# The opening of a spectral + gated-linear-unit kernel: first weights prepared by GpSimd, rows normalised by ScalarE, left-over columns split before the transpose

## The chip, the cores and the metric

The kernel runs on one core of one Trainium2 chip. The metric is the device time of one launch in microseconds (us), the median of the runs. The engines are named as in the profile: PE is TensorE (PEld its weight loads), DVE is VectorE, ACT is ScalarE, POOL is GpSimd, and SP is SyncE, whose queue issues nearly all DMAs. Each engine works through its own list of instructions in order; a list waits where its next instruction waits.

## What is computed

```python
x = A_x                                   # (1, 2048, 576)
xn = _layernorm(x, axis=-1)               # eps 1e-5, no scale or shift
g = einsum("bsd,df->bsf", xn, w_gate)     # 576 x 4608
u = einsum("bsd,df->bsf", xn, w_up)
glu = einsum("bsf,fd->bsd", sigmoid(g) * u, w_down)
spec = irfft2(rfft2(xn) * (w_r + 1j * w_i))
out = x + spec + glu
```

## The kernel before

The 2048 rows are 16 tiles of 128 rows (`NT`), taken in two passes of 8 tiles (`PAIRS`). In each pass the 4608 hidden columns are 36 units of 128 (`NF`), so there are 72 units. A unit multiplies the normalised rows with its gate and up columns by Strassen's scheme (Winograd's form): the 576 columns of x are two halves of 288 (`HD`), a pass has two halves of four tiles (512 rows, `CW`), and 7 products (`PRODS`) stand for 8. Every operand is split into a rounded high part and a low part (fp32r), so a product is 7 matmuls (`STEPS`): of the 288 columns two blocks of 128 with high and low part, and a left-over block of 32 columns (`REM`) whose high, high and low parts lie one below the other in 96 partitions (`KR`).

**Weights.** In pass 0 `make_w(f)` builds the seven 288x128 weight combinations of a unit from four raw blocks: `load_raw` (8 DMAs, L199 and L200), ACT rounds to the high part (L205, three blocks, then two and two), DVE forms the sums (L218, L220, L221) and the low parts (L207 and L209, the latter for the left-over 32 partitions). The result goes to `wsp` in DRAM, from where pass 1 reads it (`get_w`).

**Rows.** `stats` gives mean and 1/deviation of a tile (bn_stats, a square root on ACT or Newton steps, L263 to L282, on 128x1 values); `norm` (L285) is a DVE operation. `stage(p, m)` makes, for the tiles m and m+4, the seven 288-column combinations `xs`: norm twice, an ACT copy that repeats the 32 left-over columns (L307), two sums on DVE (L309, L311) and two on POOL (L310, L312). `fill(p, k, mm)` transposes combination k of two stages into `X`: 6 PE transposes (L322), an ACT copy of the high parts with 768 elements a partition (L325), and the low parts by two DVE operations (L326; L328 for the left-over columns, 32 partitions).

**Order.** The opening (L629 to L656) sends the loads of tiles 0 and 4, the identity matrices, the raw weights of unit 0, the other six tiles and the raw weights of unit 1, all from SP; then it stages m = 0, weights 0, m = 1, 2, 3, with the fills of the first half after m = 1 and unit 0 in two halves of 256 rows. `xs` has two buffers, so stages 2 and 3 reuse those of 0 and 1 when their fills are through. A scheduler places each engine's instructions; the code gives their priority. From unit 1 on, PE runs products with the down-projections (`down`, tile `po`, L598) between them. At the end of unit 35 `stage_pair` stages the four pairs of pass 1 (all four buffers at once), and `fill_ahead` fills `X` anew beside unit 36 (L678); the phases of the spectral part run beside pass 1 (L365 to L492).

Names in the profile: `xs` staged rows, `px` the transposes' PSUM tiles, `pA`, `pB`, `pE` the products' PSUM banks, `raw`, `tt`, `w` the weights, `acc` a tile of x that also takes the output, `rs` and `rstd` the statistics.

Of the kernel before, what the change touches and what calls it, by code (L numbers as in the profile page):

```python
# [9 lines left out]
F32 = mybir.dt.float32  # L10
# [6 lines left out]
P = 128  # L17
# [112 lines left out]
def spectral_glu_kernel(ctx: ExitStack, tc: tile.TileContext, x, w_r, w_i, w_gate, w_up, w_down, out):  # L130
# [3 lines left out]
    def f32(ap):  # L134
        return ap.bitcast(F32)
# [48 lines left out]
    def room(k):  # L184
        fp.close()
        R["pool"] = pool = fp.enter_context(tc.tile_pool(name=f"p{k}", bufs=1, reuse_waits="tile"))
        return pool
# [11 lines left out]
                nc.sync.dma_start(raw[:, b, :KT, :], v[h, :KT * P, cols].rearrange("(k p) f -> p k f", p=P))  # L199
                nc.sync.dma_start(raw[:, b, KT, :], v[h:h + 1, KT * P:, cols].to_broadcast([4, REM, P]))  # L200

    def parts(w, src, i, n):

        o = w[:, i:i + n]
        nc.scalar.activation(o[:, :, :3, :], src, AF.Copy)  # L205
# [3 lines left out]
        nc.vector.tensor_tensor(o[r, :, KT, :], src[r, :, KT, :], f32(o[r, :, KT, :]), op=OP.subtract)  # L209
        yield  # L210

    def make_w(f):
        raw = RAW[f]
        WS[f] = w = wpool.tile([P, NX, 5, P], F32R, tag="w", name=f"w{f}", bufs=2)
        tt = R["pool"].tile([P, 4, 3, P], F32, tag="tt", name=f"tt{f}", bufs=1)
        g = parts(w, raw[:, 1:], 0, 3)
        next(g)
        nc.vector.tensor_tensor(tt[:, :2], raw[:, :2], raw[:, 3::-3], op=OP.subtract)  # L218
        yield
        nc.vector.tensor_tensor(tt[:, 2], raw[:, 1], tt[:, 0], op=OP.subtract)  # L220
        nc.vector.tensor_tensor(tt[:, 3], raw[:, 2], tt[:, 2], op=OP.subtract)  # L221
        yield
        next(g)
        yield
        for i in (0, 2):
            yield from parts(w, tt[:, i:i + 2], 3 + i, 2)
# [29 lines left out]
    def load_x(dst, t, eng=None):  # L256
        for i, r in enumerate(rows(x, t)):
            (eng or nc.sync).dma_start(dst[i * N1:(i + 1) * N1, :D], r)

    def stats(src, t, pool, table=False):  # L260
        st = pool.tile([P, 2, 6], F32, tag="st", name=f"st{t}", bufs=2)
        for i in range(2):
            nc.vector.bn_stats(st[:, i, :], src[:, i * HD:(i + 1) * HD])  # L263
        nc.vector.bn_aggr(mv[:, t, :], st.rearrange("p a b -> p (a b)"))
        rs = pool.tile([P, 4], F32, tag="rs", name=f"rs{t}", bufs=2)
        ve, r0, w0, w1 = (rs[:, i:i + 1] for i in range(4))
        nc.vector.tensor_scalar(ve, mv[:, t, 1:2], EPS, None, op0=OP.add)
# [9 lines left out]
        nc.vector.tensor_scalar(ve, ve, -0.5, None, op0=OP.mult)  # L277
        for k in range(steps):
            nc.vector.tensor_tensor(w0, r0, r0, op=OP.mult)
            nc.vector.tensor_tensor(w0, w0, ve, op=OP.mult)  # L280
            o = rstd[:, t:t + 1] if k == steps - 1 else r0
            nc.vector.scalar_tensor_tensor(o, w0, 1.5, r0, op0=OP.add, op1=OP.mult)  # L282

    def norm(o, a, t):
        nc.vector.tensor_scalar(o, a, mv[:, t, 0:1], rstd[:, t:t + 1], op0=OP.subtract, op1=OP.mult)  # L285
# [2 lines left out]

    def stage(p, m, bufs):

        pool = R["pool"]
        XS[m] = xs = pool.tile([P, NX, (KT + 1) * P], F32, tag="xs", name=f"xs{p}_{m}", bufs=bufs)
        A11, A12, A21, A22, S1, S2, S4 = (xs[:, i] for i in range(NX))
        for i in range(2):
            t = p * TPP + i * TPC + m
            b = xs[:, 2 * i:2 * i + 2, :HD]
            if p:
                for k, r in enumerate(rows(x, t)):
                    nc.sync.dma_start(b[k * N1:(k + 1) * N1], r.rearrange("s (a d) -> s a d", a=2))
        yield  # L300
        for i in range(2):
            t = p * TPP + i * TPC + m
            b = xs[:, 2 * i:2 * i + 2, :HD]
# [3 lines left out]
        nc.scalar.activation(rem[:, :, 1:], rem[:, :, :1].to_broadcast([P, 4, 3, REM]), AF.Copy)  # L307
        yield
        nc.vector.tensor_tensor(S1, A21, A22, op=OP.add)  # L309
        nc.gpsimd.tensor_tensor(A21, A11, A21, op=OP.subtract)  # L310
        nc.vector.tensor_tensor(S2, S1, A11, op=OP.subtract)  # L311
        nc.gpsimd.tensor_tensor(S4, A12, S2, op=OP.subtract)  # L312
        yield

    def fill(p, k, mm):

        i = XA[PRODS[k][1]]
        cols = slice(2 * mm * P, (2 * mm + 2) * P)
        pt = pair(f"px{p}_{k}_{mm}")
        for j in range(2):  # L320
            for q in range(KT + 1):
                nc.tensor.transpose(pt[:, j, q * P:(q + 1) * P], XS[2 * mm + j][:, i, q * P:(q + 1) * P], idf)  # L322
        v = pt[:, :, :3 * P].rearrange("p j (q s) -> p q j s", q=3)
        o = X[:, i, :, cols].rearrange("p q (j s) -> p q j s", j=2)
        nc.scalar.activation(o[:, :3], v, AF.Copy)  # L325
        nc.vector.tensor_tensor(o[:, 3:], v[:, :KT], f32(o[:, :KT]), op=OP.subtract)  # L326
        r = slice(2 * REM, 3 * REM)
        nc.vector.tensor_tensor(o[r, KT], v[r, KT], f32(o[r, KT]), op=OP.subtract)  # L328

    def new_acc(p, m):  # L330
        t = p * TPP + m
        acc[t] = accp.tile([P, D], F32, tag=f"acc{m}", name=f"acc{t}")
        load_x(acc[t], t)

    def phase1b(t):
        pool, cf = R["pool"], R["cf"]
# [185 lines left out]
    def unit(u, beside, cols=slice(0, CW), tiles=None):  # L522
# [15 lines left out]
        def prod(i):  # L538
            b, ka, kb = PRODS[i]
            for j, (sx, sw) in enumerate(STEPS):  # L540
                k = KR if sw == KT else P
                nc.tensor.matmul(bank[b], w[:k, WB[kb], sw, :], X[:k, XA[ka], sx, cols], start=b not in seen and j == 0,  # L542
                                 stop=j == len(STEPS) - 1, skip_group_check=b in seen)
            seen.add(b)

# [93 lines left out]
    b0 = ps.tile([P, CW], F32, tag="bB", name="b0")  # L639
    for i in range(CW // P):  # L640
        nc.tensor.matmul(b0[:, i * P:(i + 1) * P], idr, idr, start=i == 0, stop=i == CW // P - 1, skip_group_check=True)
    mk = make_w(0)
    for m in range(TPC):
        for i in (m, TPC + m):
            stats(acc[i], i, R["pool"], table=True)
        sg = stage(0, m, 2)
        for _ in sg:
            pass
        if m == 0:
            for _ in mk:  # L650
                pass
        if m == 1:
            for k in range(NX):
                fill(0, k, 0)
        if m == 3:
# [28 lines left out]
    for u in range(LAST):  # L684
# [1 line left out]

        spots = {3: 1, 4: 2, 5: 1} if f % G == 0 else {1: 1, 3: 1, 4: 1, 5: 1}
        if u + 1 < LAST:
            make = make_w(u + 1) if u + 1 < NF else get_w(u + 1)
        wd = make_d(u) if u < NF else get_d(u)  # L690
        if 2 <= u < 2 + TPP:
            sides.append(later_stats(TPP + u - 2))
# [21 lines left out]
                aside()  # L714

        if u == 0:
            for k in range(NX):
                fill(0, k, 1)
            unit(0, beside, slice(CW // 2, CW), tiles)
        else:  # L720
            unit(u, beside)
# [35 lines left out]
```

## Time and profile before

| | |
|---|---|
| median of three runs | 1492.02 us (1490.39 to 1492.04) |
| the profiled execution's own time | 1491.86 us |
| its span, from the first to the last instruction | 1490.1 us |
| PE busy in the span | 1449.1 us (97%) |
| DVE busy, ACT busy, POOL busy | 959.8, 577.5 and 21.4 us |
| mean granted TensorE clock | 0.994 |

A timeline row reads: start in us from the span's first instruction, duration in us, engine, line, operation, output<-inputs, then forms (partitions x elements of one partition), the number of merged instructions, and in brackets the engine's idle time ahead of it with what ended it. A row of a view by stretches gives for each engine the busy time and the number of instructions, then the granted clock (1.00 is full), the DMA engines' busy share and GB/s. A row of a view by groups ends in "busy us, mean ns of one | idle before".

### The profile page before, as it was taken

To read this page: it belongs to the slowest core of one execution; us is meant where nothing else is said; L and a number is where in the kernel's file an instruction comes from. 1 tells how busy PE (TensorE), PEld (TensorE's weight loads), DVE (VectorE), ACT (ScalarE), POOL (GpSimd) and SP (SyncE) were. 2 spreads that over 40 slices of the span, in tenths; PEclk is the share of its full clock that TensorE was granted. 3 is DMA by queue.
4 is the path that set the end of the run, shared out by engine and by line. 5 is a ranking of instruction groups with operands and counts; after the bars stand their busy time and mean duration, and the time that the engine had idled before them with its cause. 6 is when DMAs were issued, how large, how long until landed. Compare 5 with 4: busy or idle time off the path is not lost.

```text
span 1490.1 us, 21470 instructions
## 1 busy us (share of the span) xinstructions
PE 1449.1 (97%) x8229; PEld 1276.4 (86%) x8229; DVE 959.8 (64%) x1628; ACT 577.5 (39%) x963; POOL 21.4 (1%) x36
## 2 busy tenths in 40 slices
PE   3899999999999999999999999999999999999998
PEld 3788888888888888887888888888888889899987
DVE  7988977776777777767465555456566544554544
ACT  3544433333344433334343434343444333433321
POOL 1100000000000000011000000000000000000000
PEclk9899999999999999999999999999999999999999
DMA  6477666666655666666874655486777576654522
GB/s 200 164 266 260 235 228 230 236 235 228 225 217 214 218 222 226 228 224 222 262 247 148 199 167 197 147 256 218 242 234 239 180 268 206 225 164 144 193 95 64
DMA packets 152630, 311.79 MB, mean 209 GB/s; under 512 B 14160, under 2 KB 79952, under 8 KB 147664
## 3 DMA queue, kind: packets, MB, share of 16 engines
q1 hardware_dynamic: 152528, 310.42, 61.3%
q8 instruction: 65, 1.06, 0.3%
q14 instruction: 37, 0.30, 0.1%
HBM read 189.98 MB, written 120.39 MB: 208 GB/s over the span
## 4 chain that ended last, share of the span: by engine, by line
PE 89%; DVE 6%; DMA 1%; issue 1%; SPq 1%; ACT 1%; DVEq 0%; ACTq 0%; POOL 0%; POOLq 0%
PE po L598 29%; PE pB L542 21%; PE pE L542 15%; PE pA L542 14%; PE pe L482 2%; PE pd L372 2%; PE pc L427 1%; PE pa L383 1%; PE px L322 1%; PE py L453 1%; PE pb L411 1%; DVE w L207 1%; DVE acc L603 1%; DVE X L326 1%; PE pz L465 0%
## 5 line engine op out<-in xcount | busy, mean ns | idle before, releaser
L598 PE MATMUL po<-wd,hh 128*128 128x288 f32 x2304 | 402.2, 296 | 4.3 <-DVE acc L603 2.6
L542 PE MATMUL pB<-X,w 128*128 128x512 f32 (+2 forms) x1533 | 392.9, 392 | 0.1
L603 DVE TENSOR_TENSOR acc<-acc,po 128x576 f32<-128x576 f32 x288 | 216.6, 753 | 261.1 <-PE po L598 260.2
L598 PEld LDWEIGHTS po<-wd,hh 128*128 128x128 f32 x2304 | 350.3, 189 | 25.0 <-DVE acc L603 3.9
L542 PEld LDWEIGHTS pB<-X,w 128*128 128x128 f32 (+1 forms) x1533 | 275.8, 189 | 48.8 <-ACT pB L549 0.7
L542 PE MATMUL pA<-X,w 128*128 128x512 f32 (+2 forms) x1022 | 264.3, 394 | 2.9 <-ACT X L325 1.8
L542 PE MATMUL pE<-X,w 128*128 128x512 f32 (+2 forms) x1022 | 264.0, 393 | 0.0
L598 PE MATMUL po<-wd,hl 128*128 128x288 f32 x1152 | 246.1, 294 | 0.0
L542 PEld LDWEIGHTS pA<-X,w 128*128 128x128 f32 (+1 forms) x1022 | 190.0, 190 | 41.8 <-ACT X L325 2.4
L542 PEld LDWEIGHTS pE<-X,w 128*128 128x128 f32 (+1 forms) x1022 | 185.7, 190 | 34.6 <-DVE y L563 0.5
L598 PEld LDWEIGHTS po<-wd,hl 128*128 128x128 f32 x1152 | 185.2, 188 | 0.2 <-DVE hl L584 0.2
L566 ACT ACTIVATE g<-pB 128x512 f32<-128x512 f32 (+1 forms) x73 | 43.1, 591 | 185.5 <-PE pB L542 185.0
L584 DVE TENSOR_TENSOR hl<-y,hh 128x1024 fp32r<-128x1024 f32 x72 | 88.0, 1222 | 27.6 <-ACT hh L583 27.4
L581 DVE TENSOR_TENSOR y<-y,g 128x1024 f32<-128x1024 f32 x72 | 88.3, 1226 | 5.9 <-DVE y L570 0.5
L562 ACT ACTIVATE v<-pB 128x512 f32<-128x512 f32 (+1 forms) x73 | 43.1, 591 | 120.6 <-PE pB L542 120.5
L583 ACT ACTIVATE hh<-y 128x1024 fp32r<-128x1024 f32 x72 | 75.5, 1048 | 9.0 <-DVE y L581 8.9
L570 DVE TENSOR_TENSOR y<-v,pE 128x512 f32<-128x512 f32 (+1 forms) x73 | 49.6, 680 | 45.3 <-PE pE L542 45.1
L205 ACT ACTIVATE w<-raw 128x1152 fp32r<-128x1152 f32 x36 | 42.0, 1167 | 88.2 <-PE pE L542 71.8
L563 DVE TENSOR_TENSOR y<-v,pE 128x512 f32<-128x512 f32 (+1 forms) x73 | 49.6, 679 | 37.3 <-ACT v L562 36.6
L556 ACT ACTIVATE v<-pB 128x512 f32<-128x512 f32 (+1 forms) x73 | 43.1, 590 | 65.6 <-PE pB L542 65.6
L549 ACT ACTIVATE pB<-pA 128x512 f32<-128x512 f32 (+1 forms) x73 | 42.0, 575 | 61.1 <-PE pA L542 61.0
L559 ACT ACTIVATE g<-pA 128x512 f32<-128x512 f32 (+1 forms) x73 | 43.2, 592 | 53.5 <-PE pA L542 53.4
(121 smaller groups left out, 1311.2 us busy)
## 6 DMA issues: line engine op xcount, KB each, us to landing
wsp<-w SPq DMA_DIRECT2D x36, 2240.0 KB
w<-wsp SPq DMA_DIRECT2D x252, 320.0 KB
wdsp<-wd SPq DMA_DIRECT2D x36, 576.0 KB
wd<-wdsp SPq DMA_DIRECT2D x36, 576.0 KB
std<-in_B_w_down SPq DMA_DIRECT2D x36, 288.0 KB
raw<-in_B_w_gate SPq DMA_DIRECT2D x72, 128.0 KB
raw<-in_B_w_up SPq DMA_DIRECT2D x72, 128.0 KB
sc<-x SPq DMA_DIRECT2D x16, 290.0 KB
```

The source lines that it names most:

```text
L542: nc.tensor.matmul(bank[b], w[:k, WB[kb], sw, :], X[:k, XA[ka], sx, cols], start=b not in seen and j == 0, stop=j == len(STEPS) - 1, skip_ ...
L556: nc.scalar.activation(v[:, 0], bank["B"], AF.Copy)
L559: nc.scalar.activation(g[:, 0], bank["A"], AF.Sigmoid)
L562: nc.scalar.activation(v[:, 1], bank["B"], AF.Copy)
L563: nc.vector.tensor_tensor(y[:, 1], v[:, 1], bank["E"], op=OP.add)
L566: nc.scalar.activation(g[:, 1], bank["B"], AF.Sigmoid)
L570: add = lambda: nc.vector.tensor_tensor(y[:, 0], v[:, 0], bank["E"], op=OP.add)
L581: nc.vector.tensor_tensor(Y, Y, G_, op=OP.mult)
L583: ends.extend([first, lambda: nc.scalar.activation(hh, Y, AF.Copy), lambda: nc.vector.tensor_tensor(hl, Y, f32(hh), op=OP.subtract)])
L584: lambda: nc.vector.tensor_tensor(hl, Y, f32(hh), op=OP.subtract)])
L598: nc.tensor.matmul(pd[:, b, :HD], l[:, c, cols], w[:, k, b * HD:(b + 1) * HD], start=g == 0 and l is hh and k == 0, stop=g == G - 1 and l ...
L603: nc.vector.tensor_tensor(a, a, pd[:, :, :HD], op=OP.add)
```

## The change

The subtractions of `make_w` for units 0 and 1 go from DVE to POOL (`eng`); all of `make_w(0)` is placed ahead of the staging. `stats` takes the two tiles of a stage together (128x2 values). In pass 0 ACT normalises (Identity with scale `rstd` and bias `nmr`, a new DVE product), and the two sums that POOL made are DVE's; in pass 1 norm stays on DVE and those two sums on POOL. The left-over columns of all seven combinations are split into high, high and low parts in `rm` ahead of the transpose (an ACT copy with 448 elements, L326, and a DVE subtraction with 224, L327), so that `fill` has four fp32 transposes and two of `rm` (L338, L339), two ACT copies (L342, L344) and one DVE operation (L343). The products read 128 instead of 96 partitions of the left-over block; POOL clears the other 32 of `X` at the start. Tiles 1 and 5 are loaded from ACT's queue, and the identity matrices behind the raw weights.

```diff
+    nmr = fix.tile([P, TPP], F32, name="nmr")
...
-    def parts(w, src, i, n):
+    def parts(w, src, i, n, eng):
         o = w[:, i:i + n]
         nc.scalar.activation(o[:, :, :3, :], src, AF.Copy)
         yield
-        nc.vector.tensor_tensor(o[:, :, 3:, :], src[:, :, :KT, :], f32(o[:, :, :KT, :]), op=OP.subtract)
+        eng.tensor_tensor(o[:, :, 3:, :], src[:, :, :KT, :], f32(o[:, :, :KT, :]), op=OP.subtract)
...
-    def make_w(f):
+    def make_w(f, eng=nc.vector):
...
-    def stats(src, t, pool, table=False):
+    def stats(srcs, t0, step, pool, table=False):
...
+        if table:
+            nc.vector.scalar_tensor_tensor(nmr[:, ts], mv[:, ts, 0], -1.0, rstd[:, ts], op0=OP.mult, op1=OP.mult)
...
-            norm(b, b if p else acc[t].rearrange("p (a d) -> p a d", a=2), t)
-
-        rem = xs[:, :4, KT * P:].rearrange("p a (q r) -> p a q r", q=4)
-        nc.scalar.activation(rem[:, :, 1:], rem[:, :, :1].to_broadcast([P, 4, 3, REM]), AF.Copy)
-        yield
+            if p:
+                norm(b, b, t)
+            else:
+                nc.scalar.activation(b, acc[t].rearrange("p (a d) -> p a d", a=2), AF.Identity,
+                                     bias=nmr[:, t:t + 1], scale=rstd[:, t:t + 1])
+        yield
+        eng = nc.gpsimd if p else nc.vector
         nc.vector.tensor_tensor(S1, A21, A22, op=OP.add)
-        nc.gpsimd.tensor_tensor(A21, A11, A21, op=OP.subtract)
+        eng.tensor_tensor(A21, A11, A21, op=OP.subtract)
         nc.vector.tensor_tensor(S2, S1, A11, op=OP.subtract)
-        nc.gpsimd.tensor_tensor(S4, A12, S2, op=OP.subtract)
+        eng.tensor_tensor(S4, A12, S2, op=OP.subtract)
+        yield
+        rem = xs[:, :, KT * P:]
+        nc.scalar.activation(rm[:, :, :2], rem.unsqueeze(2).to_broadcast([P, NX, 2, REM]), AF.Copy)
+        nc.vector.tensor_tensor(rm[:, :, 2], rem, f32(rm[:, :, 0]), op=OP.subtract)
         yield
...
-            for q in range(KT + 1):
-                nc.tensor.transpose(pt[:, j, q * P:(q + 1) * P], XS[2 * mm + j][:, i, q * P:(q + 1) * P], idf)
...
-        nc.scalar.activation(o[:, :3], v, AF.Copy)
-        nc.vector.tensor_tensor(o[:, 3:], v[:, :KT], f32(o[:, :KT]), op=OP.subtract)
-        r = slice(2 * REM, 3 * REM)
-        nc.vector.tensor_tensor(o[r, KT], v[r, KT], f32(o[r, KT]), op=OP.subtract)
+            xs, rm = XS[2 * mm + j]
+            for q in range(KT):
+                nc.tensor.transpose(pt[:, 0, (2 * q + j) * P:(2 * q + j + 1) * P], xs[:, i, q * P:(q + 1) * P], idf)
+            nc.tensor.transpose(pt[:KR, 1, j * P:(j + 1) * P].bitcast(F32R), rm[:, i].rearrange("p a b -> p (a b)"), idr)
+        v = pt[:, 0].rearrange("p (q s) -> p q s", q=KT)
+        o = X[:, i, :, cols]
+        nc.scalar.activation(o[:, :KT], v, AF.Copy)
+        nc.vector.tensor_tensor(o[:, KT + 1:], v, f32(o[:, :KT]), op=OP.subtract)
+        nc.scalar.activation(o[:KR, KT], pt[:KR, 1, :2 * P], AF.Copy)
...
-                k = KR if sw == KT else P
-                nc.tensor.matmul(bank[b], w[:k, WB[kb], sw, :], X[:k, XA[ka], sx, cols], start=b not in seen and j == 0,
+                nc.tensor.matmul(bank[b], w[:, WB[kb], sw, :], X[:, XA[ka], sx, cols], start=b not in seen and j == 0,
...
+    nc.gpsimd.memset(f32(X[KR:, :, KT, :]), 0.0)
     for m in range(TPC):
         for i in (m, TPC + m):
-            new_acc(0, i)
+            new_acc(0, i, nc.scalar if m == 1 else nc.sync)
         if m == 0:
+            load_raw(0)
             nc.sync.dma_start(idf, con["id"])
             load_r(idr, con["id"])
-            load_raw(0)
     load_raw(1)
...
-    mk = make_w(0)
+    for _ in make_w(0, nc.gpsimd):
+        pass
     for m in range(TPC):
-        for i in (m, TPC + m):
-            stats(acc[i], i, R["pool"], table=True)
-        sg = stage(0, m, 2)
-        for _ in sg:
+        stats([acc[m], acc[TPC + m]], m, TPC, R["pool"], table=True)
+        for _ in stage(0, m, 2):
             pass
...
-            make = make_w(u + 1) if u + 1 < NF else get_w(u + 1)
+            make = make_w(u + 1, nc.vector if u else nc.gpsimd) if u + 1 < NF else get_w(u + 1)
```

How this moves the instructions, at three places. ACT's list at the start of the program, before (`rs0` and `rs4` are the statistics of tiles 0 and 4, `w0` and `raw0` the weights of unit 0, `xs0_0` and `xs0_1` the stages of m = 0 and m = 1):

```order
L269 ACT_TABLE_LOAD
L269 ACTIVATE rs0_208<-rs0_208 128x1
L269 ACTIVATE rs4_220<-rs4_220 128x1
L307 ACTIVATE xs0_0_228<-xs0_0_228 128x4x96
L205 ACTIVATE w0_236<-raw0_163 128x3x384
L205 ACTIVATE w0_236<-tt0_237 128x2x384 x2
L269 ACTIVATE rs1_255<-rs1_255 128x1
```

And now:

```order
L259 DMA acc1_174<-in_A_x 64x576 x2
L259 DMA acc5_177<-in_A_x 64x576 x2
L274 ACT_TABLE_LOAD
L274 ACTIVATE rs0_228<-rs0_228 128x2
L274 ACTIVATE rs1_254<-rs1_254 128x2
L206 ACTIVATE w0_206<-raw0_163 128x3x384
L316 ACTIVATE xs0_0_237<-acc0_157,nmr_65,rstd_64 128x576
L206 ACTIVATE w0_206<-tt0_207 128x2x384
L316 ACTIVATE xs0_0_237<-acc4_160,nmr_65,rstd_64 128x576
L206 ACTIVATE w0_206<-tt0_207 128x2x384
L316 ACTIVATE xs0_1_263<-acc1_174,nmr_65,rstd_64 128x576
L316 ACTIVATE xs0_1_263<-acc5_177,nmr_65,rstd_64 128x576
```

The first rounding of the weights, which needs `raw0`, now stands ahead of all four normalisations, and the third rounding, which needs `tt0`, ahead of the last two.

POOL's list at the same place, now (before, POOL has only two sums of 384 elements for each stage there):

```order
L645 MEMSET X_66 32x7x512
L219 ISA
L219 TENSOR_TENSOR tt0_207<-raw0_163 128x768
L208 TENSOR_TENSOR w0_206<-raw0_163,w0_206 128x3x256
L221 TENSOR_TENSOR tt0_207<-raw0_163,tt0_207 128x384
L210 TENSOR_TENSOR w0_206<-raw0_163,w0_206 32x3x128
L222 TENSOR_TENSOR tt0_207<-raw0_163,tt0_207 128x384
L208 TENSOR_TENSOR w0_206<-tt0_207,w0_206 128x2x256
L210 TENSOR_TENSOR w0_206<-tt0_207,w0_206 32x2x128
```

The operation that makes the last `tt0` (L222) is the fifth in POOL's list; two more for `w0` follow, and then nine for `w1`.

ACT's list at the end of pass 0, before, from the staging of pass 1 (`xs1_`) to the first fill (`px1_0_`):

```order
L307 ACTIVATE xs1_0_5969<-xs1_0_5969 128x4x96
L556 ACTIVATE v35_5945<-pB35_0_5948 128x512
L559 ACTIVATE g35_5944<-pA35_0_5947 128x512
L307 ACTIVATE xs1_1_5974<-xs1_1_5974 128x4x96
L562 ACTIVATE v35_5945<-pB35_0_5948 128x512
L307 ACTIVATE xs1_2_5979<-xs1_2_5979 128x4x96
L566 ACTIVATE g35_5944<-pB35_0_5948 128x512
L307 ACTIVATE xs1_3_5984<-xs1_3_5984 128x4x96
L325 ACTIVATE X_65<-px1_0_0_6139 128x3x256
```

And now:

```order
L326 ACTIVATE rm1_0_5948<-xs1_0_5947 128x7x64
L571 ACTIVATE v35_5923<-pB35_0_5926 128x512
L326 ACTIVATE rm1_1_5954<-xs1_1_5953 128x7x64
L574 ACTIVATE g35_5922<-pA35_0_5925 128x512
L577 ACTIVATE v35_5923<-pB35_0_5926 128x512
L326 ACTIVATE rm1_2_5960<-xs1_2_5959 128x7x64
L581 ACTIVATE g35_5922<-pB35_0_5926 128x512
L326 ACTIVATE rm1_3_5966<-xs1_3_5965 128x7x64
L342 ACTIVATE X_66<-px1_0_0_6125 128x2x256
```

In the place of the copy that needs the norm alone (four of the seven combinations) stands one that reads all seven.

More of the change, by code (lines that the diff above doesn't have):

```diff
@@ L258, in load_x @@
             (eng or nc.sync).dma_start(dst[i * N1:(i + 1) * N1, :D], r)
-    def stats(src, t, pool, table=False):
[L261 to L267, printed above, removed]
+    def stats(srcs, t0, step, pool, table=False):
+        n = len(srcs)
+        ts = slice(t0, t0 + (n - 1) * step + 1, step)
+        st = pool.tile([P, n, 2, 6], F32, tag="st", name=f"st{t0}", bufs=2)
+        for k, src in enumerate(srcs):
+            for i in range(2):
+                nc.vector.bn_stats(st[:, k, i, :], src[:, i * HD:(i + 1) * HD])
+            nc.vector.bn_aggr(mv[:, t0 + k * step, :], st[:, k].rearrange("p a b -> p (a b)"))
+        rs = pool.tile([P, 4, n], F32, tag="rs", name=f"rs{t0}", bufs=2)
+        ve, r0, w0, w1 = (rs[:, i] for i in range(4))
+        nc.vector.tensor_scalar(ve, mv[:, ts, 1], EPS, None, op0=OP.add)
         if table:
@@ L641, in spectral_glu_kernel @@
         nc.tensor.matmul(b0[:, i * P:(i + 1) * P], idr, idr, start=i == 0, stop=i == CW // P - 1, skip_group_check=True)
[L642 removed]
+    for _ in make_w(0, nc.gpsimd):
+        pass
     for m in range(TPC):
[L644 to L651 removed]
+        stats([acc[m], acc[TPC + m]], m, TPC, R["pool"], table=True)
+        for _ in stage(0, m, 2):
+            pass
+        if m % 2:
+            for k in range(NX):
+                fill(0, k, m // 2)
         if m == 1:
[L653 to L655 removed]
             tiles = unit(0, lambda i: None, slice(0, CW // 2))
@@ L716, in spectral_glu_kernel @@
         if u == 0:
-            for k in range(NX):
-                fill(0, k, 1)
             unit(0, beside, slice(CW // 2, CW), tiles)
```

33 lines of the change are left out of this document (16 added, 17 removed).

## The prediction

> **What bounds the kernel now.** I read the page first, then the stretches of the opening, then the timeline of the opening and of the passage from pass 0 to pass 1, since the change touches no other place.
>
> ```profile
> span 1490.1 us, 21470 instructions
> PE 89%; DVE 6%; DMA 1%; issue 1%; SPq 1%; ACT 1%; DVEq 0%; ACTq 0%; POOL 0%; POOLq 0%
> 20.00:30.00 10.00, 4.51 (x18) 3.49 (x19) 9.81 (x47) 2.85 (x7) 2.34 (x2) 1.00 0.90 312
> 30.00:40.00 10.00, 7.24 (x59) 6.75 (x59) 9.16 (x26) 8.88 (x16) 0.00 (x0) 1.00 0.28 82
> 40.00:50.00 10.00, 7.08 (x30) 5.52 (x28) 9.52 (x20) 3.59 (x7) 3.30 (x4) 0.50 0.13 38
> 50.00:60.00 10.00, 9.93 (x65) 9.10 (x65) 8.41 (x16) 4.80 (x9) 0.95 (x1) 0.82 0.42 157
> 60.00:70.00 10.00, 10.00 (x50) 8.08 (x49) 9.55 (x15) 7.39 (x12) 0.00 (x0) 1.00 0.76 255
> ```
>
> PE is 89% of the chain, and busy 10.00 of 10 us from 60 us on. Only ahead of 60 us is it idle, and there DVE is full (9.81, 9.16, 9.52 of 10), and the TensorE clock is 0.50 from 40 to 50 us. So the change is worth what it shifts in the first 60 us and at the passage, where the profile shows PE waiting again; the rest follows unchanged. Most of the opening's price hangs on when the first product starts:
>
> ```profile
> 8.29 5.39 DMA raw<-in_B_w_up
> 13.93 1.16 ACT L205 ACTIVATE w<-raw 128x1152 fp32r<-128x1152 f32 x1 [4.33 <-DMA acc<-in_A_x]
> 13.97 0.96 DVE L218 TENSOR_TENSOR tt<-raw 128x768 f32<-128x768 f32 x1 [3.19 <-DMA raw<-in_B_w_up]
> 14.99 0.83 ACT L205 ACTIVATE w<-tt 128x768 fp32r<-128x768 f32 x1
> 19.29 0.41 DVE L209 TENSOR_TENSOR w<-tt,w 32x256 fp32r<-32x256 f32 x1
> 25.91 0.54 DVE L309 TENSOR_TENSOR xs<-xs 128x384 f32<-128x384 f32 x1
> 27.06 1.94 PE L542 MATMUL pA<-X,w 128*128 128x256 f32 x5
> 36.12 0.85 PE L322 MATMUL px<-idf,xs 128*128 128x128 f32 x6
> 48.12 0.58 PE L542 MATMUL pA<-X,w 128*128 128x256 f32 x1 [0.90 <-ACT X L325]
> ```
>
> The raw weights land at 8.29 + 5.39 = 13.68 us; DVE makes w0 from 13.97 to 19.70 (5.7 us) and only then stages m = 1; the first product starts at 27.06, the first half's last fill stands at 36.12, the second half starts at 48.12.
>
> **The opening, step by step.** What goes from DVE: 5.7 us for w0, as much for w1, eight norms, and the left-over subtraction in each of 14 fills. The place of w0 is taken by POOL, and this is what POOL and DVE do side by side:
>
> ```profile
> 11.60 0.99 POOL L312 TENSOR_TENSOR xs<-xs 128x384 f32<-128x384 f32 x1
> 24.35 0.15 DVE L279 TENSOR_TENSOR rs<-rs 128x1 f32<-128x1 f32 x1
> 41.67 0.55 DVE L311 TENSOR_TENSOR xs<-xs 128x384 f32<-128x384 f32 x1
> 41.78 1.29 POOL L310 TENSOR_TENSOR xs<-xs 128x384 f32<-128x384 f32 x1 [12.91 <-DVE rs L277]
> 42.14 0.95 DVE L279 TENSOR_TENSOR rs<-rs 128x1 f32<-128x1 f32 x1
> 48.22 0.69 DVE L326 TENSOR_TENSOR X<-px,X 128x512 fp32r<-128x512 f32 x1
> 48.45 1.00 POOL L310 TENSOR_TENSOR xs<-xs 128x384 f32<-128x384 f32 x1 [4.43 <-DVE xs L309]
> 48.82 1.04 DVE L311 TENSOR_TENSOR xs<-xs 128x384 f32<-128x384 f32 x1
> ```
>
> The sum L311 takes 0.55 us with POOL held up, and 1.04 us beside a POOL operation that ends at 49.45; it ends 0.42 after that. POOL's operation that begins 0.11 after DVE's L311 takes 1.29 in place of 0.99. The tiny L279 takes 0.95 in place of 0.15. L326, which reads PSUM, keeps its 0.69. So on operands in SBUF the two take turns: each waits for the other's running operation. Hence DVE's ten such operations for stages 0 and 1 stand between POOL's.
>
> POOL's price: 0.99 us for 384 elements, 2.58 ns each. The nine operations for one unit (768, 768, 384, 384, 384, 512, 256, 512, 256) are 4224 elements: 10.9 us. Below, DVE's 5.7 us is a floor; above, no row shows POOL write fp32r or work on 32 partitions, so I keep 30% more (14.2) as the other end. I take 10.9, since the row nearest in kind is POOL's own.
>
> The Trainium skill, GPSIMD Engine Reference, "Performance versus the Vector engine", gives 4497 ns for a 2048-element tensor_tensor, from which I estimate 9.3 us for the nine. With that the sum below would be about 1.5 us lower. The row of 0.99 us decides; no run shows another size.
>
> Arrival: the raw loads leave up to 1.1 us earlier (the identity loads of 0.6 and 0.4 us of issue are behind them), but four more row loads are under way from ACT's queue. I take 13.4 us, between 12.6 and 14.2. The statistics are over by then (before, DVE waited 3.19 us for raw), so sharing the small operations wins nothing: the weights hide it. POOL's clearing of X (3584 elements, by the same 2.58 ns 9.2 us) ends near 10 us, hidden too; ACT's four issues end long before.
>
> Now the lists. POOL's L219 (768) runs 13.4 to 15.4. ACT: first rounding to 14.6, a norm (0.7, as for its 576-element copy below) to 15.3, second rounding (0.83, waits for L219) to 16.2, norm to 16.9. POOL's L208 is on until 17.4. Then turns: DVE L320 (288 elements, 0.45 by the 0.54 for 384) 17.85, POOL L221 18.85, DVE L321 and L322 19.75, POOL L210 20.75, DVE L323 21.2, POOL L222 22.2. Only now can ACT round for the third time (23.0) and normalise tiles 1 and 5 (24.4). POOL L208, L210, L208 are on until 25.5. DVE L320 25.95, POOL L210 26.6, DVE L327 and L321 27.5, POOL L219 of w1 29.5, DVE L322 29.95, POOL L221 30.95, DVE L323 31.4, ACT's `rm` copy 32.0, DVE's last split behind POOL's L222 32.8; transposes 0.3, ACT's copy into X 0.6. **The first product starts at 33.7 us instead of 27.06: 6.7 us later.**
>
> ```profile
> 35.86 0.81 ACT L325 ACTIVATE X<-px 128x768 fp32r<-128x768 f32 x1 [0.90 <-PE px L322]
> 38.35 0.42 DVE L328 TENSOR_TENSOR X<-px,X 32x256 fp32r<-32x256 f32 x1
> 39.05 0.39 ACT L562 ACTIVATE v<-pB 128x256 f32<-128x256 f32 x1
> 39.31 0.70 ACT L244 ACTIVATE wd<-std 128x576 fp32r<-128x576 f32 x1
> ```
>
> From there on the intervals are much as before. A fill costs ACT 0.6 + 0.39 in place of 0.81 (2.5 us more over 14 fills) and DVE 0.42 less. The second half still waits until the last fill frees the two staging buffers, and then for the whole chain of norm, sums and split: 12.0 us before (36.12 to 48.12), 12 to 14 now, as four ACT norms stand in a row with the fills' copies. I set DVE's relief against that and give back 0.7: **opening +6**. Bounds: if POOL and DVE never blocked each other, L222 would end at 20.3, the first product would start near 27, and the lighter DVE could win 4: -4. With POOL 30% dearer and raw at 14.2, two dozen turns are longer: +11.
>
> The products' 96 rows become 128. I cost that at nothing, as the forms last alike:
>
> ```profile
> L542 PE MATMUL pB<-X,w 128*128 128x512 f32 x1278 | 333.5, 394 | 0.0
> L542 PE MATMUL pB<-X,w 96*128 96x512 f32 x213 | 84.2, 395 | 0.0
> ```
>
> **The passage to pass 1.** Here DVE still normalises and POOL makes two sums of each stage.
>
> ```profile
> 674.30 0.53 ACT L307 ACTIVATE xs<-xs 128x384 f32<-128x384 f32 x1 [1.93 <-DVE xs L285]
> 674.77 1.48 PE L322 MATMUL px<-idf,xs 128*128 128x128 f32 x12
> 676.97 1.98 POOL L312 TENSOR_TENSOR xs<-xs 128x384 f32<-128x384 f32 x1
> 677.20 0.49 PE L542 MATMUL pA<-X,w 128*128 128x512 f32 x1 [0.95 <-ACT X L325]
> 679.27 0.84 PE L322 MATMUL px<-idf,xs 128*128 128x128 f32 x6 [1.58 <-DVE X L328]
> ```
>
> The first fill needed only norm and copy (674.83), while POOL's last sum ended at 678.95. Now every fill needs `rm`, which reads all seven combinations, so POOL's last sum comes ahead of it, then 0.6 (ACT), 0.4 (DVE) and the handovers: 680.1 instead of about 676.2 for the last transposes of the first fill, 3.9 later. In that time DVE works off the products that made PE wait 1.58 us at 679.27, which gives back about 1: **+3**, between 0 (both waits hidden anew) and +6 (four stages in one list, each with its own handovers).
>
> **Sum.** 1491.86 (the profiled execution, 1.76 over its span) + 6 + 3 = 1500.9. That execution stands 0.16 under the median of 1492.02, so on the median it is 1501.0 us, 0.6% slower. Differences within 0.2% (3 us) can't be told from no change here.
>
> **Rivals.**
>
> Faster, 0.08: the turns cost little and DVE's relief decides. It falls to this if the first product starts before about 27 us, that is if POOL's list runs through by 20.3 for L222. Then the nine w1 operations that DVE drops shorten the 12.0 us to the second half, the stretch at half clock ends sooner, -4 for the opening, and the passage is hidden: 1488. For it: DVE full in all three stretches. Against it: 1.04 for 0.55 and 0.95 for 0.15, and ACT's list, where tt0 stands ahead of the norms.
>
> Same, 0.13: the turns are as worked out, but DVE's relief gives nearly all back in the second half, and the passage is +1: 1493. For it: nine w1 operations, 5.7 us, gone between 32 and 57. Against it: the second half waits on a chain, in which DVE has two more handovers.
>
> Dearer, 0.16: the clock. Before, at 40 to 50 us, waits of PE of under 2 us each go with a clock of 0.50. If PE's longer waits now bring a second such stretch, at the passage, where PE waits about 4 us, or in the opening, half clock over 10 us of work costs up to 5: 1506. The same price follows if POOL is 30% dearer.
>
> The Trainium skill, TensorE: Matmul & The Clock Gate, "The HAM clock gate", says the clock halves after one idle window of about 3.4 us. By that rule the passage, idle about 4 us, would fall to half clock and the time would be near 1505; the trace is no clean witness, as its half clock came with shorter waits.
>
> Forecast, 0.63: 1497 to 1504.
>
> **Numbers.** 1501, range 1490 to 1509: it takes in the forecast, the dearer case and the rival "same", and leaves out the faster one and the tail above. Slower by over 0.2%: 0.63 + 0.16 + a small part of "same" (0.02) = 0.81; same 0.11; faster 0.08.
>
> **What would show it.** In the changed profile: L206 with `raw` on ACT near 13.4 with the norms behind it; POOL's nine w0 operations over more than 10.9 us; DVE's L320 to L323 lasting well over 0.45 while POOL is on; the first L557 product near 34 and the first of the second half near 55; the first fill's last transposes of pass 1 about 4 us later against pass 0's end. It is wrong if POOL's 768-element operation is far from 2 us, if L320 to L323 stay at 0.45 beside POOL, or if raw lands by 11.

## The result, and the profile after

| | before | changed |
|---|---|---|
| median of 12 runs each | 1491.72 us (1490.39 to 1493.30) | 1492.48 us (1490.58 to 1495.51) |
| ratio of the times, 95% interval | | 1.0005 [0.9997, 1.0012] |
| profiled execution, own time and span | 1491.86, 1490.1 us | 1490.94, 1489.1 us |

No difference that can be measured; the forecast was 9 us slower. The page of the changed kernel has this row (busy us, share of the span, instructions):

```profile
PE 1439.7 (97%) x8229; PEld 1273.9 (86%) x8229; DVE 939.2 (63%) x1570; ACT 587.4 (39%) x995; POOL 35.4 (2%) x47
```

PE runs as many matmuls as before, but is busy 9.4 us less (1449.1 before). The losses of the opening and the passage were there all the same, so something was won elsewhere. First the opening, by the view of stretches and the timeline of the changed kernel:

```profile
20.00:30.00 10.00, 1.32 (x6) 0.91 (x6) 8.26 (x11) 3.03 (x5) 8.97 (x8) 1.00 0.52 207
40.00:50.00 10.00, 6.49 (x43) 5.89 (x41) 4.91 (x11) 9.10 (x17) 4.20 (x5) 0.83 0.49 197
50.00:60.00 10.00, 7.17 (x40) 6.40 (x41) 5.22 (x11) 4.54 (x10) 0.00 (x0) 0.66 0.76 243
```

```profile
13.53 1.16 ACT L206 ACTIVATE w<-raw 128x1152 fp32r<-128x1152 f32 x1 [2.36 <-DMA idf<-c_id]
13.59 1.82 POOL L219 TENSOR_TENSOR tt<-raw 128x768 f32<-128x768 f32 x1 [9.78 <-DMA idf<-c_id]
...
20.68 1.48 POOL L208 TENSOR_TENSOR w<-tt,w 128x512 fp32r<-128x512 f32 x1
20.96 0.45 DVE L268 BATCH_NORM_STATS2 st<-acc 128x6 f32<-128x288 f32 x1
...
23.15 1.46 DVE L320 TENSOR_TENSOR xs<-xs 128x288 f32<-128x288 f32 x1 [1.74 <-ACT xs L316]
24.38 0.81 POOL L210 TENSOR_TENSOR w<-tt,w 32x256 fp32r<-32x256 f32 x1
...
25.27 1.84 POOL L219 TENSOR_TENSOR tt<-raw 128x768 f32<-128x768 f32 x1
25.36 2.06 DVE L321 TENSOR_TENSOR xs<-xs 128x288 f32<-128x288 f32 x1
32.49 0.58 PE L557 MATMUL pA<-X,w 128*128 128x256 f32 x1 [0.58 <-ACT X L342]
54.07 0.58 PE L557 MATMUL pA<-X,w 128*128 128x256 f32 x1 [0.58 <-ACT X L342]
```

L321 begins 0.09 us after POOL's L219 and lasts until 0.31 after it: 2.06 us for 288 elements. Not every DVE operation is held up: L268, a statistics operation with one input, keeps its 0.45 us inside POOL's L208. The first product starts at 32.49 (27.06 before), the second half at 54.07 (48.12 before).

How far the changed kernel lies behind can be read at the last sigmoid of each unit, on ACT (L566 before, L581 now). At unit 4 and unit 34 of the kernel before, and then of the changed kernel:

```profile
124.00 0.60 ACT L566 ACTIVATE g<-pB 128x512 f32<-128x512 f32 x1 [5.63 <-PE pB L542]
654.10 0.60 ACT L566 ACTIVATE g<-pB 128x512 f32<-128x512 f32 x1 [4.21 <-PE pB L542]
```

```profile
126.33 0.60 ACT L581 ACTIVATE g<-pB 128x512 f32<-128x512 f32 x1 [4.19 <-PE pB L557]
652.23 0.60 ACT L581 ACTIVATE g<-pB 128x512 f32<-128x512 f32 x1 [4.19 <-PE pB L557]
```

It is 2.3 us behind after the opening and 1.9 ahead 30 units later: 4.2 us won where the forecast saw nothing happen, 0.14 in every unit. PE has no gap there. What differs is the step from one product to the next where products follow each other (seven matmuls in a row, merged). Before, and then now:

```profile
321.38 1.77 PE L542 MATMUL pA<-X,w 128*128 128x512 f32 x7
322.99 1.78 PE L542 MATMUL pE<-X,w 128*128 128x512 f32 x7
324.60 1.78 PE L542 MATMUL pB<-X,w 128*128 128x512 f32 x7
```

```profile
322.16 1.75 PE L557 MATMUL pA<-X,w 128*128 128x512 f32 x7
323.75 1.75 PE L557 MATMUL pE<-X,w 128*128 128x512 f32 x7
325.33 1.75 PE L557 MATMUL pB<-X,w 128*128 128x512 f32 x7
```

A product starts every 1.61 us before and every 1.59 us now. One matmul lasts nearly as long (392 or 393 ns now, 394 or 395 before), but they overlap, so their lengths say nothing of their spacing.

The passage to pass 1 in the changed kernel:

```profile
671.59 1.77 PE L557 MATMUL pE<-X,w 128*128 128x512 f32 x7
675.14 0.78 POOL L323 TENSOR_TENSOR xs<-xs 128x288 f32<-128x288 f32 x1
675.95 0.58 ACT L326 ACTIVATE rm<-xs 128x448 fp32r<-128x448 f32 x1 [3.51 <-POOL xs L323]
676.56 0.39 DVE L327 TENSOR_TENSOR rm<-xs,rm 128x224 fp32r<-128x224 f32 x1 [2.04 <-ACT rm L326]
676.87 0.75 DVE L618 TENSOR_TENSOR acc<-acc,po 128x576 f32<-128x576 f32 x1
677.67 0.69 PE L338 MATMUL px<-idf,xs 128*128 128x128 f32 x2 [3.75 <-DVE acc L618]
679.68 0.79 PE L557 MATMUL pA<-X,w 128*128 128x512 f32 x1 [0.69 <-ACT X L342]
```

From the last product of pass 0 to the first of pass 1 it takes 679.68 - 671.59 = 8.1 us; before, that product began at 673.16 and the first of pass 1 at 677.20: 4.0. DVE waits for the last split L327, which waits for ACT and for POOL's last sum, and the addition L618 stands behind L327 in DVE's list; PE needs the PSUM that L618 sets free. And the clock falls:

```profile
670.00:680.00 10.00, 5.57 (x33) 4.61 (x31) 7.14 (x13) 3.09 (x6) 3.16 (x4) 0.82 0.80 291
680.00:690.00 10.00, 9.58 (x56) 8.15 (x56) 5.66 (x9) 6.78 (x15) 0.00 (x0) 0.83 0.43 165
```

### The profile page after: what moved, and what is told of

Read it like the earlier page. It is cut to its first block, busy times and chain, and to the rows that moved or that the text cites. A ratio compares the mean times of both kernels' runs of the same rounds, so it can differ in the third digit from the quotient of the medians.

```text
span 1489.1 us, 21432 instructions
## 1 busy us (share of the span) xinstructions
PE 1439.7 (97%) x8229; PEld 1273.9 (86%) x8229; DVE 939.2 (63%) x1570; ACT 587.4 (39%) x995; POOL 35.4 (2%) x47
## 4 chain that ended last, share of the span: by engine, by line
PE 92%; DVE 2%; DMA 2%; ACT 2%; issue 1%; SPq 1%; POOL 1%; ACTq 0%; POOLq 0%; DVEq 0%
PE po L613 30%; PE pB L557 23%; PE pE L557 15%; PE pA L557 15%; PE pe L498 2%; PE pd L388 2%; PE pc L443 1%; PE pa L399 1%; PE px L338 1%; PE pb L427 1%; PE py L469 1%; DMA xb<-in_A_x 1%; PE pz L481 0%; SPq L308 0%; PE pf L373 0%
## 5 line engine op out<-in xcount | busy, mean ns | idle before, releaser
L557 PE MATMUL pB<-X,w 128*128 128x512 f32 (+1 forms) x1533 | 389.7, 390 | 2.6 <-ACT v L577 2.6
L618 DVE TENSOR_TENSOR acc<-acc,po 128x576 f32<-128x576 f32 x288 | 216.5, 752 | 224.7 <-PE po L613 223.9
L557 PEld LDWEIGHTS pB<-X,w 128*128 128x128 f32 x1533 | 274.6, 188 | 51.4 <-ACT v L577 3.9
L557 PE MATMUL pA<-X,w 128*128 128x512 f32 (+1 forms) x1022 | 261.0, 391 | 1.8 <-ACT X L342 1.8
L557 PE MATMUL pE<-X,w 128*128 128x512 f32 (+1 forms) x1022 | 261.8, 392 | 0.0
L557 PEld LDWEIGHTS pA<-X,w 128*128 128x128 f32 x1022 | 189.9, 190 | 38.8 <-ACT X L342 2.6
L557 PEld LDWEIGHTS pE<-X,w 128*128 128x128 f32 x1022 | 186.0, 190 | 33.2 <-ACT X L342 0.4
L581 ACT ACTIVATE g<-pB 128x512 f32<-128x512 f32 (+1 forms) x73 | 43.2, 592 | 179.8 <-PE pB L557 179.3
```

The source lines that it names most:

```text
L557: nc.tensor.matmul(bank[b], w[:, WB[kb], sw, :], X[:, XA[ka], sx, cols], start=b not in seen and j == 0, stop=j == len(STEPS) - 1, skip_gr ...
L581: nc.scalar.activation(g[:, 1], bank["B"], AF.Sigmoid)
L618: nc.vector.tensor_tensor(a, a, pd[:, :, :HD], op=OP.add)
```

## The experiments

Theory: the 128 rows of the left-over product win what GpSimd's work loses in the opening and at the passage. The main rival: the lighter DVE wins it, as the forecast's rival "same" had it. Each run is compared with runs of the kernel before on the same chip:

| run | median, us | before, us | ratio [95% interval] |
|---|---|---|---|
| e1 changed, 96 rows | 1499.87 | 1491.80 | 1.0049 [1.0035, 1.0063] |
| e2 before, 128 rows | 1488.62 | 1491.80 | 0.9974 [0.9965, 0.9983] |
| e3 changed, both weights on DVE | 1486.67 | 1491.80 | 0.9963 [0.9951, 0.9976] |
| e4 changed, old form in pass 1 | 1489.59 | 1491.80 | 0.9982 [0.9973, 0.9991] |
| f1 e3 and e4 together | 1480.57 | 1492.73 | 0.9918 [0.9905, 0.9931] |
| f2 changed, two matmuls of 96 rows | 1504.45 | 1492.73 | 1.0073 [1.0059, 1.0088] |
| f4 changed, unit 1 on DVE | 1487.76 | 1492.73 | 0.9968 [0.9956, 0.9980] |
| f5 changed, unit 0 on DVE | 1487.53 | 1492.73 | 0.9962 [0.9948, 0.9976] |
| f3 e3, sums of pass 1 on DVE | 1479.37 | 1493.41 | 0.9911 [0.9897, 0.9924] |
| f7 f1, sums of pass 1 on DVE | 1481.10 | 1493.41 | 0.9920 [0.9907, 0.9932] |
| f6 changed, sums of pass 1 on DVE | 1487.22 | 1493.97 | 0.9956 [0.9942, 0.9969] |
| g1 before, all sums on DVE | 1494.19 | 1493.97 | 1.0002 [0.9992, 1.0011] |

In the expectations the two halves of unit 0 are counted apart, so that their units 5, 35 and 36 are units 4, 34 and 35 here; and their distances are 0.3 us too low, since they were not taken from the start of each span.

### The row count: e1, e2, f2

```diff
-                nc.tensor.matmul(bank[b], w[:, WB[kb], sw, :], X[:, XA[ka], sx, cols], ...
+                k = KR if sw == KT else P
+                nc.tensor.matmul(bank[b], w[:k, WB[kb], sw, :], X[:k, XA[ka], sx, cols], ...
```

> The changed kernel, only that the left-over product reads 96 partitions again instead of 128. In the two traces the changed kernel lies 4.4 us behind at unit 0, 2.0 behind at unit 5 and 2.2 ahead at unit 35, so it wins 0.14 us in every unit of pass 0 and some 0.07 in every unit of pass 1: about 6.5 us in all. Theory (rows: a matmul of another row count between the others makes PE slip): the gain goes, 1499, and the slope between unit 5 and unit 35 is nil against the kernel before. Rival (the gain comes from the lighter DVE or the shared statistics): 1492.5, with the slope kept.

1499.87. The sigmoids of units 4 and 34 in this run:

```profile
127.42 0.60 ACT L582 ACTIVATE g<-pB 128x512 f32<-128x512 f32 x1 [4.21 <-PE pB L558]
657.51 0.60 ACT L582 ACTIVATE g<-pB 128x512 f32<-128x512 f32 x1 [4.21 <-PE pB L558]
```

They are 3.4 us behind the kernel before at both places: the slope is gone, and the time is 7.4 us above the changed kernel's by the medians, 6.6 by the ratios. The rows made the gain.

The counterpart puts the 128 rows into the kernel before, which has them nowhere:

```diff
+        nc.gpsimd.memset(xs[:, :4, KT * P + KR:], 0.0)
...
-        nc.scalar.activation(rem[:, :, 1:], rem[:, :, :1].to_broadcast([P, 4, 3, REM]), AF.Copy)
+        nc.scalar.activation(rem[:, :, 1:3], rem[:, :, :1].to_broadcast([P, 4, 2, REM]), AF.Copy)
...
-                k = KR if sw == KT else P
-                nc.tensor.matmul(bank[b], w[:k, WB[kb], sw, :], X[:k, XA[ka], sx, cols], ...
+                nc.tensor.matmul(bank[b], w[:, WB[kb], sw, :], X[:, XA[ka], sx, cols], ...
```

> The kernel before, only that the left-over product reads 128 partitions; GpSimd clears the fourth copy of the left-over columns at the start of each stage, so that those partitions of X hold zero. Theory (rows): 1491.7 - 6.5 = 1485, since opening and passage stay as before. Rival (DVE or statistics): 1491.7, or up to 0.5 over it for the clearing.

1488.62: half of what was expected. The sigmoids of units 4 and 34 show the same slope (from 2.6 us behind to 1.6 ahead), and ACT's rows of the opening show a loss that the expectation left out:

```profile
126.63 0.60 ACT L566 ACTIVATE g<-pB 128x512 f32<-128x512 f32 x1 [4.74 <-PE pB L542]
652.51 0.60 ACT L566 ACTIVATE g<-pB 128x512 f32<-128x512 f32 x1 [4.19 <-PE pB L542]
```

```profile
41.57 1.28 ACT L269 ACT_TABLE_LOAD   x1
44.66 1.28 ACT L566 ACT_TABLE_LOAD   x1
```

The edit moved a square root behind the first sigmoid in ACT's list. The kernel before loads a table twice in its opening, this one four times. Another 1.3 us go between units 34 and 36, at the passage, where the clock of this execution is 0.94 and 0.89 in two stretches of 10 us (1.00 in both before). So in pass 0 the rows are worth the same in both kernels; what the two loads cost by themselves was not measured.

f2 asks whether PE pays for each matmul of 96 rows or for the change of rows; it leaves 32 of 128 columns out of one more matmul, the one just ahead:

```diff
+                k = KR if j >= len(STEPS) - 2 else P
```

> The changed kernel with 96 rows in the last two matmuls of every product (the left-over one, and the one ahead of it, which leaves out 32 of its 128 columns of x, so the output differs). With 96 rows in the last matmul alone the kernel took 1499.9 against 1492.5. If PE pays where the row count changes, two neighbours cost what one does: 1500. If it pays for each matmul of 96 rows: 1507.

1504.45, between the two; the kernel before was 0.9 us higher beside it than beside e1, so it is some 3.7 above e1. Between units 4 and 34 (127.59 and 659.99 against 124.00 and 654.10) it loses 2.3 us where one 96-row matmul costs 4.2. A neighbour costs about half of the first, so neither of the two simple pictures holds. Why PE slips is not settled.

```profile
127.59 0.60 ACT L582 ACTIVATE g<-pB 128x512 f32<-128x512 f32 x1 [4.22 <-PE pB L558]
659.99 0.60 ACT L582 ACTIVATE g<-pB 128x512 f32<-128x512 f32 x1 [4.22 <-PE pB L558]
```

### GpSimd in the opening: e3, f4, f5

```diff
-    for _ in make_w(0, nc.gpsimd):
+    for _ in make_w(0):
...
-            make = make_w(u + 1, nc.vector if u else nc.gpsimd) if u + 1 < NF else get_w(u + 1)
+            make = make_w(u + 1) if u + 1 < NF else get_w(u + 1)
```

> The changed kernel with the weights of units 0 and 1 on DVE again. Theory (turns between POOL and DVE make the late start): the first product starts some 4 us earlier, near 28.5 instead of 32.5, and of the 4.4 us behind at unit 0 about 3 go: 1489.5. Rival (ACT's list and the split that needs all seven combinations make it late, and DVE is the fuller): the first product stays near 32.5 and the time at 1492.5 or above.

1486.67, 5.8 us under the changed kernel, twice what the theory gave. The same sums in the timeline of this run, and the first product:

```profile
20.55 0.44 DVE L321 TENSOR_TENSOR xs<-xs 128x288 f32<-128x288 f32 x1
20.91 0.45 DVE L322 TENSOR_TENSOR xs<-xs 128x288 f32<-128x288 f32 x1
25.74 0.58 PE L557 MATMUL pA<-X,w 128*128 128x256 f32 x1 [0.58 <-ACT X L342]
```

Every sum lasts 0.44 to 0.46 us. In the changed kernel eight DVE operations between 17.5 and 29.5 us (two of them quoted above) last together 6.5 us longer than here, and the first product starts 6.75 later. So GpSimd's share of the weights is the opening's price, and DVE, though it has 11.4 us more to do for two units, is the faster engine for them. The turns are not all of it: in the changed kernel DVE also stands idle for 1.74 us ahead of L320 at 23.15, behind ACT's norms, which stand behind a rounding that needs GpSimd's `tt`. No run parts the two.

f4 takes back unit 1 alone (the second line pair above), f5 unit 0 alone (the first).

> The changed kernel with the weights of unit 1 alone back on DVE; unit 0 stays on GpSimd. Theory (the turns beside the second stage's sums are the price, and those are taken with the operations for unit 1): first product near 28, and most of the 5.8 us comes back: 1488. Rival (GpSimd's longer list for unit 0 and what waits for it on ACT are the price): first product still over 31, 1491 to 1492.5.

> The changed kernel with the weights of unit 0 alone back on DVE; unit 1 stays on GpSimd. With both on DVE the second stage's sums ended at 23.6 us, before the raw weights of unit 1 are there, and DVE was busy 10.00 of 10 us between 20 and 30. So here GpSimd's operations stand beside the fills, whose DVE operations read PSUM and were not held up in any trace so far. Theory (turns are taken only on operands in SBUF): 1486.7 or up to 2 us under it. Rival (any DVE operation beside GpSimd is held up): over 1488.5.

1487.76 and 1487.53, by their ratios no slower than e3: within the intervals, either half of GpSimd's work taken away brings back as much as both. The single executions in the traces don't bear this out to the full: e3 is 2.2 and 2.6 us ahead of them at unit 34 (8.3 ahead of before, against 6.1 and 5.7), and its span is still 2.2 and 2.5 us shorter (1484.9 against 1487.1 and 1487.4). The first product starts at 29.81 in f4, between the 28 of the theory and the 31 of the rival, so GpSimd's list for unit 0 has a price without unit 1 too; in f5 it starts at 27.14. The expectation of f5 that GpSimd would meet only the fills was wrong:

```profile
24.00 1.80 POOL L219 TENSOR_TENSOR tt<-raw 128x768 f32<-128x768 f32 x1 [20.20 <-DVE st L268]
24.24 1.81 DVE L327 TENSOR_TENSOR rm<-xs,rm 128x224 fp32r<-128x224 f32 x1
27.14 0.58 PE L557 MATMUL pA<-X,w 128*128 128x256 f32 x1 [0.58 <-ACT X L342]
29.62 1.65 DVE L272 TENSOR_SCALAR rs<-mv 128x2 f32<-128x2 f32 x1
31.18 0.68 DVE L343 TENSOR_TENSOR X<-px,X 128x512 fp32r<-128x512 f32 x1
```

L327, the split ahead of the first product, meets one 768-element operation and lasts 1.81 instead of 0.39: one meeting moves the first product by 1.4 (27.14 against 25.74). L343, which reads PSUM, keeps its 0.68 beside POOL's next operations.

### The passage: e4, f1, f3, f6, f7, g1

e4 has two helpers with the bodies of before's `stage` and `fill` (and e2's clearing), and pass 1 calls them:

```diff
-        gs = [stage(1, m, TPC) for m in range(TPC)]
+        gs = [stage_o(1, m, TPC) for m in range(TPC)]
...
-                fill(1, k, mm)
+                fill_o(1, k, mm)
```

> The changed kernel, with the stages and fills of pass 1 alone written as before (left-over columns split behind the transpose; the fourth copy cleared to zero). Theory (the split ahead of the transpose makes the first fill of pass 1 wait for all seven sums): the 2.0 us that the changed kernel loses between units 35 and 36 go, and the stretch at half clock there with them: 1490.5. Rival (the sums on GpSimd, which both forms have, or the later end of unit 35 make it): 1492.5.

1489.59. From the last product of pass 0 to the first of pass 1 it takes 4.1 us again. The half clock, expected to go as well, only grows shorter: 0.83 from 670 to 680 us and 1.00 from there. f1 has this edit and e3's:

> Both edits of the two runs before it together: the weights of units 0 and 1 on DVE, and pass 1 staged and filled as before; the 128 rows, ACT's norms and the split ahead of the transpose in pass 0 stay. If the opening and the passage are separate costs, the two gains add: 1492.5 - 5.8 - 2.9 = 1483.8. If both runs only won the same wait (the passage's wait moves with the end of pass 0), it stays near 1486.5.

1480.57, a larger gain than the sum of the two: e3 had made the passage worse, with a clock of 0.51 from 670 to 680 us (rows below), and f1 keeps it at 1.00. f3 leaves the new form and takes GpSimd out of it; it is e3 with

```diff
-        eng = nc.gpsimd if p else nc.vector
+        eng = nc.vector
```

> The kernel with both units' weights on DVE (1486.7), and also the two sums that GpSimd makes of each stage of pass 1 on DVE. At the passage PE waits 3.8 us in one piece there, for an addition on DVE that stands behind the split of the last stage, which waits for GpSimd's last sum. Theory (GpSimd's sum of about 1 us ahead of the split, with its turns, makes that wait): it falls to some 2.5 us, and with it the stretch at half clock of 10.2 us: 1483 to 1485. Rival (DVE has no room at the passage, so that 3.7 us more on it cost as much as they save): 1486.5 to 1488.

1479.37, the fastest kernel here: 0.9% under before, 7.3 us under e3, at least twice what was expected. The passage of e3 and then of f3:

```profile
665.15 1.77 PE L557 MATMUL pE<-X,w 128*128 128x512 f32 x7
671.25 0.69 PE L338 MATMUL px<-idf,xs 128*128 128x128 f32 x2 [3.76 <-DVE acc L618]
673.26 0.79 PE L557 MATMUL pA<-X,w 128*128 128x512 f32 x1 [0.69 <-ACT X L342]
```

```profile
663.94 1.77 PE L557 MATMUL pE<-X,w 128*128 128x512 f32 x7
664.24 0.75 DVE L618 TENSOR_TENSOR acc<-acc,po 128x576 f32<-128x576 f32 x1
667.75 0.50 PE L557 MATMUL pA<-X,w 128*128 128x512 f32 x1 [0.69 <-ACT X L342]
```

In f3 the addition L618 is through 6.2 us earlier (it ended at 671.20 in e3), the wait of 3.76 is gone, and the interval is 3.8 instead of 8.1 us. The rest goes with the clock, in the stretch 670 to 680 us, e3 first:

```profile
670.00:680.00 10.00, 7.64 (x31) 6.07 (x31) 6.63 (x9) 4.88 (x11) 0.00 (x0) 0.51 0.76 285
```

```profile
670.00:680.00 10.00, 10.00 (x70) 8.61 (x68) 5.08 (x9) 8.00 (x17) 0.00 (x0) 1.00 0.75 267
```

f6 is the changed kernel with f3's edit alone:

> The changed kernel with only the sums of pass 1 on DVE; the weights of units 0 and 1 stay on GpSimd. With both weights on DVE this edit was worth 7.3 us (1486.7 to 1479.4). If the passage's price stands apart from the opening's: 1492.5 - 7.3 = 1485, PE's wait of 3.7 us at the passage gone and the clock full there. If it was won only because DVE was ahead by then: above 1489.

1487.22, a ratio of 0.9956 against the changed kernel's 1.0005: again some 7 us by the ratios (5.3 by the medians; the kernel before took 1493.97 beside this run), and the interval is 3.8. The price of the passage stands apart from the opening's. But the clock does not come back wholly:

```profile
670.00:680.00 10.00, 8.26 (x48) 6.96 (x47) 8.16 (x15) 5.67 (x11) 0.00 (x0) 0.84 0.82 289
676.82 0.67 PE L338 MATMUL px<-idf,xs 128*128 128x128 f32 x2 [1.04 <-ACT X L344]
```

The last two test how far the rule goes, on f1 and on the kernel before:

```diff
-        nc.gpsimd.tensor_tensor(A21, A11, A21, op=OP.subtract)
+        nc.vector.tensor_tensor(A21, A11, A21, op=OP.subtract)
...
-        nc.gpsimd.tensor_tensor(S4, A12, S2, op=OP.subtract)
+        nc.vector.tensor_tensor(S4, A12, S2, op=OP.subtract)
```

> The fastest kernel so far (1480.6: weights on DVE, pass 1 staged and filled as before) with the same edit: GpSimd's sums of pass 1 on DVE. There the first fill does not wait for them, and PE's longest wait at the passage is 1.1 us. Theory: nothing to win, 4.4 us more on DVE: 1480.5 to 1483. Rival (GpSimd's turns hold DVE up by more than that): under 1480.

> The kernel before with GpSimd's two sums of every stage, in both passes, on DVE. Theory (a GpSimd operation costs DVE about its own length wherever DVE has operands in SBUF to work on): DVE gets 16 operations of 0.55 us, 8.8 us, and loses the turns; before 60 us DVE is full, so the balance is near nil: 1490 to 1493. Rival (GpSimd helps where DVE is full): 1494 or more. Second rival (any GpSimd operation there costs more than it takes over): under 1489.

f7 took 1481.10, as the first theory had it, with a ratio of 0.9920 against f1's 0.9918: where the first fill does not wait for GpSimd's sums, it makes no measurable difference which engine makes them. g1 took 1494.19, above the theory's 1490 to 1493 and inside the range of its first rival. But the kernel before took 1493.97 beside it, and the ratio of 1.0002 is the nil balance of the theory. It is a weak witness all the same, as its opening has the two more table loads of e2.

## Why the prediction was wrong

**The step that failed** is "The products' 96 rows become 128. I cost that at nothing, as the forms last alike". The rows quoted for it give the length of one matmul, 394 and 395 ns, and matmuls overlap, so equal lengths were no reason for nothing. The timeline of before had the spacing (a product every 1.61 us), but no product of 128 rows throughout to set beside it; the term needed a range. Taking the 128 rows away costs 7.4 us (e1). With -7.4 in the place of nothing the forecast's sum is 1493.6. And e1, which is the changed kernel without this term, is 8.1 us slower than the kernel before (1499.87 against 1491.80), where the two other terms together forecast 9; in its trace it is 3.4 us behind at unit 4, for the +6, and 6.6 at unit 36, past the passage.

**POOL's price** was right: the nine operations for unit 0 take 11.3 us of POOL (from L219 at 13.59 to the end of the last L210 at 25.19, with 0.3 of gaps), 10.9 forecast. The 768-element one takes 1.82, not 2.0. That X's clearing ends at 3.8 us and not near 10 changed nothing.

**The turns** were right, and so were the places: first product 32.49 (33.7 forecast), second half 54.07 (near 55), and L343 on PSUM untouched. The rule for this in the Trainium skill, SBUF — State Buffer, "Who interferes with whom", is that a DVE instruction with two SBUF inputs contends with a GpSimd instruction that reads SBUF, and that the lock is an exclusive one. The trace of f5 agrees: L327, with two inputs, takes 1.81 us for 0.39 beside an operation of 1.80.

**The opening's +6** was too large for what stays: 4.8 us at the sigmoid of the first half of unit 0, 2.3 at unit 4. Of the difference some 0.6 is the rows (0.14 a unit), and 1.6 goes between units 3 and 4, where PE waits in the kernel before and not in the changed one. The prediction had PE full from 60 us on and left this wait out; no run takes it apart:

```profile
120.49 0.79 PE L598 MATMUL po<-wd,hh 128*128 128x288 f32 x4 [1.16 <-DVE acc L603]
```

GpSimd's help hid a gain: e3, with all the weights on DVE, is 4.1 us ahead of the kernel before at unit 4, and the same two items are some 2.2 of that. That the rest is the relief of DVE which the rival "faster" counted on is likely, but no run shows it alone.

**The passage's +3** was right in its mechanism and nearly in its size: the interval grows by 4.1 us (3.9 forecast); at the last sigmoid of unit 36 about 1.9 of them have been given back (0.3 behind there, 1.9 ahead at unit 34). L618 behind L327 was not foreseen: it, not the fill itself, ends the wait.

**The clock.** The stretch at half clock at the passage, which the rival "dearer" had, came: 0.82 and 0.83 in two stretches, that is 3.5 us of work lost at most. In the opening it shrank: 0.83 and 0.66 for 0.50 and 0.82. The rule in the Trainium skill, TensorE: Matmul & The Clock Gate, "The HAM clock gate", is half clock after one idle window of about 3.4 us. The traces here do not fit it throughout, and give no other rule. The changed kernel and e3 have the half clock with one wait of 3.75, but in e3 it is there from 670.0 on, 2.5 us after that wait began (671.25 - 3.76 = 667.49). f6 has 0.84 with no wait over 1.04 and e4 0.83 with none over 1.10, while f1, with the same two waits as e4 (0.90 and 1.10), has 1.00. So a long single wait is not needed, and what decides stays open. These are single executions, and the mean granted clock of one kernel varies: the kernel before, beside f6, took 1491.92 us at 0.998 and 1496.76 at 0.992.

**The rival "same"** gave 1493, close to the result, for another reason: it wanted the relief of DVE to make up for the turns. e1 shows that without the rows the changed kernel is 0.5% slower, so that rival falls too.

## What to carry to other kernels

Cost a matmul by the step to the next one in a run of them, never by its own length: a single operand of another row count in a series of full ones made every product 1.3% longer, and rows of zeros made it good. Before work goes to GpSimd, list which DVE operations with operands in SBUF will run beside it, those with two inputs above all, and what stands behind them: a meeting can cost DVE nearly a whole GpSimd operation (1.4 of 1.80 us for L327 in f5). When a large change moves the time little, undo its parts one by one: here the change without GpSimd's share, apart from the clearing of X (f3), is 0.9% faster, and the whole change is no faster at all.

## What the runs showed of the hardware that was not expected

- A 96-row matmul among 128-row ones (512 columns, fp32r) delays what follows: 1.61 us from one product of seven matmuls to the next instead of 1.59, at nearly the same length of each matmul (395 against 394 ns). A second 96-row matmul beside it costs about half as much again (2.3 us over 30 units where the first costs 4.2, f2).
- GpSimd clears fast and adds slowly: 3584 elements a partition, on 32 partitions, in 3.08 us (0.86 ns each), against 1.82 us for a sum of 768 (2.4 ns each) and 1.09 for one of 384.
- A DVE operation on 128x2 values can be held up by GpSimd like the large ones: L272 took 1.65 us in f5, beside a POOL operation of 1.82, and 0.15 to 0.17 without one. It has a single input, like L268, which kept its 0.45 us beside POOL in the changed kernel; why the two differ was not tested.
- A reordering by which a square root falls behind the first sigmoid costs two table loads of 1.28 us on ACT (e2).
